# First token tile's layer norm in two groups of two blocks, and the first weights' low parts on GpSimd

## The chip, the core and the metric

The kernel runs on one core of a Trainium2 chip. The metric is the device time of one execution in microseconds (us). A core has a matmul engine (PE, TensorE), three engines for element-wise work (DVE = VectorE, ACT = ScalarE, POOL = GpSimd) and SyncE (SP), whose queue issues most of the transfers here. Each engine works through its own instructions in order, and waits at an instruction until all that it needs is there.

## The reference, cut to what matters

`x` is 2048 tokens by 640. It is normalised once, and the result goes both to an attention with 32 heads of 128 over 512 cached keys, and to a dense layer with a squared relu of width 1728. The output is gated.

```python
xn = _layernorm(x, axis=-1)                 # (x - mean) / sqrt(var + 1e-5)
q = xn @ wq                                 # 32 heads of 128
s = softmax(q @ k.T * 128 ** -0.5) @ v @ wo # per head, the last 512 cached positions
h = relu(xn @ w1 + b1) ** 2
g = silu(h @ w2 + b2)
return x + s * g
```

All arrays are float32.

## The kernel before

PE multiplies in a rounded float32 type (`F32R`). To keep the accuracy, each operand is kept as two tensors: a high part, which is a copy rounded by ACT (`activation(hi, src, AF.Copy)`), and a low part, the difference to the source (`tensor_tensor(lo, src, hi, op=subtract)`). A product of two such operands is three matmuls (`products`, L92 to L97): high by high (L95), high by low (L96), low by high (L97).

The tokens are cut into four tiles of 512 (`NT`), and each tile into four blocks of 128 rows. First the dense layer runs over tiles 0 to 2, each over 14 chunks of the width 1728 (13 of 128 and one of 64, which stands fourth). The attention follows, over all four tiles; the dense layer of tile 3 is spread over it. Attention is written out by a plan of due times that the change does not touch.

**The first tile.** `ln_first` (L200) calls `ln_stats(0)` (L132): four transfers of `x` (L144), and on DVE the statistics of each block (`bn_stats` in two halves, `bn_aggr`). After the fourth block, for all four at once, epsilon is added, ACT takes the square root (L154), and DVE makes the reciprocal and one Newton step of four small instructions. Then DVE normalises the four blocks in place. PE transposes them, 20 times 128x128, into five banks `px0` to `px4` (L205). `load_w(0, dve)` loads and splits the weights of chunk 0. ACT copies each bank to the high part `xT` (L210), DVE takes the low part; these ten instructions feed the first up-projection. For tiles 1 and 2, `ln_stats` and `ln_chunk` do the same work in another form during the tile before.

**The weights.** The weights of a chunk are loaded while tile 0 runs and stay. `load_w(f)` (L218) issues the transfer of the chunk's `w1` (to `w1r`, L221) and of its `w2` (to `w2r`, L226) on SP; then ACT makes the high parts (L231, L233) and an engine, DVE in every case, the low parts (L232, L234). `w1r` and `w2r` share a pool tag with two buffers, so the `w1r` of a chunk may be issued only when the `w1r` of the chunk before has been read by both engines, and `w2r` likewise.

**The first tile's loop.** `mlp_step(n)` emits the up-projection of chunk n and then the down-projection of chunk n-1. Up (`ph`): 15 matmuls, then ACT's relu `r` (L278), GpSimd's square (L237), ACT's high part `h` (L238) and DVE's low part (L239). Down (`py`): 15 matmuls that read h and `w2`.

**The order of the instructions.** An engine that is wrapped in `Ordered` (`pe`, `dve`, `act`, `pool`, `sp`; all its calls are recorded at L72) keeps the order in which the program states its instructions. Calls by `nc.` names are placed by a scheduler between them, by its own estimates. In `ln_first` before, DVE's work is ordered; ACT's, PE's and SP's is placed.

Of the kernel before, what the change touches and what calls it, by code (L numbers as in the profile page):

```python
# [8 lines left out]
F32 = mybir.dt.float32  # L9
F32R = mybir.dt.float32r  # L10
AF = mybir.ActivationFunctionType
# [3 lines left out]
P = 128  # L15
# [5 lines left out]
def kernel(  # L21
# [67 lines left out]
    def raw(ap):  # L89
        return ap.bitcast(F32)  # L90
# [39 lines left out]
    def ln_tile(t, b):  # L130
        tag = "stage" if t or b < 2 else "mr"
        return xp.tile([P, D], F32, tag=tag, name=f"xb{t}_{b}")  # L132

    def ln_stats(t):
# [24 lines left out]
        dve.tensor_tensor(r, r, y, op=ALU.mult)  # L159
        if t == 0:  # L160
            for b in range(NB):
                dve.tensor_scalar(
                    xn[b],
                    xn[b],
                    mv[:, 0, b : b + 1],
                    mv[:, 1, b : b + 1],
                    op0=ALU.subtract,
                    op1=ALU.mult,
                )
        xs = [  # L170
# [4 lines left out]
        ]  # L175
        return xn if t == 0 else mv, xs

# [22 lines left out]
    def ln_first():  # L200
        xn, xs = ln_stats(0)
        pts = [ps_y.tile([P, NT], F32, tag="py", name=f"px0_{c}") for c in range(DC)]
        for b in range(NB):
            for c in range(DC):
                nc.tensor.transpose(  # L205
                    pts[c][:, b * P : (b + 1) * P], xn[b][:, c * P : (c + 1) * P], ident
                )
        load_w(0, dve)
        for c in range(DC):
            nc.scalar.activation(xs[0][:, c, :], pts[c], AF.Copy)  # L210
            dve.tensor_tensor(xs[1][:, c, :], pts[c], raw(xs[0][:, c, :]), op=ALU.subtract)
        return xs
# [4 lines left out]

    def load_w(f, engine=nc.vector):  # L218
        f0, n = chunks[f]
# [5 lines left out]
        for k in range(0, P, n):  # L225
            nc.sync.dma_start(wb[k : k + n, :], w2[f0 : f0 + n, :])  # L226
        if n < P:
            w1p = [w1s[f][0][:, :, i * n : (i + 1) * n] for i in range(2)]
        else:
            w1p = w1s[f]  # L230
        nc.scalar.activation(w1p[0], wa[:, :, :n], AF.Copy)  # L231
        engine.tensor_tensor(w1p[1], wa[:, :, :n], raw(w1p[0]), op=ALU.subtract)  # L232
        nc.scalar.activation(w2s[f][0], wb, AF.Copy)  # L233
        engine.tensor_tensor(w2s[f][1], wb, raw(w2s[f][0]), op=ALU.subtract)  # L234

# [797 lines left out]
```

## Time and profile before

| | |
|---|---|
| time, median of 3 runs | 2020.71 us (2017.9 to 2021.19) |
| time of the profiled execution | 2021.47 us |
| its span, first to last instruction | 2019.7 us |
| granted TensorE clock, mean | 0.999 |
| busy: PE, DVE, POOL, ACT | 98%, 76%, 68%, 49% of the span |
| first transpose; first matmul of the up-projection | 12.53; 16.90 us |

A row of the timeline has the start, the length (both in us), the engine, the line, the operation, what it writes and reads with its shape, and in brackets how long the engine was idle before it and what ended that. A row of the waits has who waited for whom, the sum in us, how often, and the longest. A row of the windows has the window and its length, the busy time of PE, weight load, DVE, ACT and POOL with the number of instructions, the granted clock, the share of the transfer engines and GB/s. Rows of groups have the count, then the busy time and the mean in ns.

### The profile page before, as it was taken

The page shows a single profiled execution, that of the slowest core. Times are in us where ns is not written, and L with a number is a line of the kernel's source. Part 1 is how long each engine was busy: PE and PEld are TensorE (multiplying, and loading weights), DVE is VectorE, ACT ScalarE, POOL GpSimd, SP SyncE. Part 2 cuts the span into 40 slices and gives each one's busy share as a digit, 9 for nine tenths or more (in the row PEclk, how much of TensorE's full clock was granted, in tenths as well). Part 3 has the DMA queues.
Part 4 walks back from the last instruction along what each step waited for, and adds up shares of the span by engine and source line. Part 5 has one row for each costly group of instructions (what it writes and reads, how often), then busy time and mean ns, then how long its engine had stood idle before and what let it go on. Part 6 is the DMA issues. An engine that isn't in the chain of part 4 may idle for free.

```text
span 2019.7 us, 25025 instructions
## 1 busy us (share of the span) xinstructions
PE 1987.9 (98%) x8832; PEld 1609.3 (80%) x8832; DVE 1535.8 (76%) x2252; ACT 985.8 (49%) x1266; POOL 1375.4 (68%) x754
## 2 busy tenths in 40 slices
PE   7999999999999999999999999999999999999998
PEld 6788887788888888888887788787878888788877
DVE  5532337788888888888887778888888888888864
ACT  4432335555555555555554455555555555555533
POOL 1121227788777777777777788788888888877841
PEclk9999999999999999999999999999999999999999
DMA  4431454322333332333335433333333333333344
GB/s 140 128 113 29 177 196 132 99 90 89 90 89 89 90 89 90 90 91 90 91 96 159 154 95 105 110 110 111 110 110 111 110 112 110 96 91 90 106 146 140
DMA packets 126862, 220.32 MB, mean 109 GB/s; under 512 B 21542, under 2 KB 36304, under 8 KB 125456
## 3 DMA queue, kind: packets, MB, share of 16 engines
q1 hardware_dynamic: 123744, 204.28, 33.6%
q0 software_dynamic: 2992, 14.43, 1.8%
q8 instruction: 70, 1.15, 0.2%
q14 instruction: 56, 0.46, 0.1%
HBM read 194.26 MB, written 24.39 MB: 108 GB/s over the span
## 4 chain that ended last, share of the span: by engine, by line
PE 88%; DMA 6%; DVE 2%; POOL 1%; ACT 1%; issue 1%; SPq 0%; POOLq 0%; DVEq 0%
PE pq L72 20%; PE r L72 19%; PE s L72 17%; PE o L72 15%; DMA bm<-m_d 2%; PE py L96 2%; PE py L97 2%; PE py L95 2%; PE ph L96 2%; PE ph L95 2%; PE ph L97 2%; PE ly L72 2%; DMA m_d<-rowm 1%; PE lu L72 1%; DMA w1r<-in_w_dram 1%; DVE e L72 1%
## 5 line engine op out<-in xcount | busy, mean ns | idle before, releaser
L72 POOL TENSOR_TENSOR pt<-e,pt 128x1024 fp32r<-128x1024 f32 x256 | 617.5, 2412 | 296.1 <-ACT pt L72 296.1
L72 PE MATMUL r<-ot,wo 128*128 128x512 f32 x1920 | 496.9, 389 | 0.5 <-DVE acc L72 0.5
L72 PE MATMUL pq<-ax,wq 128*128 128x512 f32 x1920 | 473.1, 396 | 0.1
L72 ACT ACTIVATE e<-e 128x1024 f32<-128x1024 f32 x256 | 269.5, 1053 | 370.6 <-DVE e L72 331.6
L72 PEld LDWEIGHTS r<-ot,wo 128*128 128x128 f32 x1920 | 360.2, 188 | 75.9 <-DVE acc L72 0.9
L72 PEld LDWEIGHTS pq<-ax,wq 128*128 128x128 f32 x1920 | 350.9, 188 | 84.5 <-DMA ax<-xT_d 0.9
L72 PE MATMUL o<-pt,wv 128*128 128x512 f32 x1536 | 386.5, 398 | 0.4 <-POOL pt L72 0.3
L72 PE MATMUL s<-q,wk 128*128 128x512 f32 x1536 | 372.2, 391 | 9.1 <-DVE e L72 9.0
L72 DVE TRANSPOSE_TENSOR_REDUCE rdm<-s 128x32 f32<-128x1024 f32 x256 | 319.3, 1249 | 60.6 <-PE s L72 46.3
L72 PEld LDWEIGHTS s<-q,wk 128*128 128x128 f32 x1536 | 286.4, 188 | 76.9 <-DVE e L72 16.3
L72 PEld LDWEIGHTS o<-pt,wv 128*128 128x128 f32 x1536 | 278.7, 188 | 70.8 <-POOL pt L72 1.5
L72 DVE TENSOR_TENSOR e<-s,bm 128x1024 f32<-128x1024 f32 x256 | 299.9, 1212 | 37.5 <-DMA bm<-m_d 33.7
L72 POOL TENSOR_TENSOR su<-e,e 128x1024 f32<-128x1024 f32 x128 | 308.5, 2410 | 0.0
L72 ACT ACTIVATE pt<-e 128x1024 fp32r<-128x1024 f32 x256 | 271.7, 1061 | 7.8
L72 DVE TENSOR_TENSOR acc<-r,acc 128x512 f32<-128x512 f32 x300 | 202.5, 675 | 2.8 <-PE r L72 2.8
L237 POOL TENSOR_TENSOR r<-r 128x512 f32<-128x512 f32 (+1 forms) x42 | 44.1, 1049 | 227.5 <-ACT r L278 207.9
L72 ACT ACTIVATE ot<-o 128x512 fp32r<-128x512 f32 x128 | 76.8, 600 | 228.3 <-DVE o L72 228.3
L72 DVE TRANSPOSE_TENSOR_REDUCE rds<-su 128x32 f32<-128x1024 f32 x128 | 158.5, 1239 | 10.7 <-POOL su L72 9.0
L72 ACT ACTIVATE q<-pq 128x512 fp32r<-128x512 f32 x128 | 76.7, 599 | 164.8 <-PE pq L72 164.7
L72 DVE TENSOR_TENSOR ot<-o,ot 128x512 fp32r<-128x512 f32 x128 | 88.5, 691 | 32.0 <-ACT ot L72 32.0
L239 DVE TENSOR_TENSOR h<-r,h 128x512 fp32r<-128x512 f32 (+1 forms) x42 | 29.0, 690 | 107.7 <-ACT h L238 107.6
L72 POOL TENSOR_TENSOR wq<-qr,wq 128x640 fp32r<-128x640 f32 x62 | 98.5, 1588 | 4.0 <-ACT wq L72 2.8
(122 smaller groups left out, 2152.6 us busy)
## 6 DMA issues: line engine op xcount, KB each, us to landing
bm<-m_d SPq DMA_DIRECT2D x128, 256.0 KB, 3.3
bs<-s_d SPq DMA_DIRECT2D x128, 256.0 KB, 4.0
qr<-in_wq_dram SPq DMA_DIRECT2D x64, 320.0 KB, 4.4
or<-in_wo_dram SPq DMA_DIRECT2D x64, 320.0 KB, 4.5
kr<-in_kT_dram SPq DMA_DIRECT2D x64, 256.0 KB, 4.4
vr<-in_v_dram SPq DMA_DIRECT2D x64, 256.0 KB, 4.3
xT_d<-xT POOLq DMA_DIRECT2D x6, 1280.0 KB, 7.5
xb<-in_x_dram SPq DMA_DIRECT2D x16, 320.0 KB, 3.5
```

The lines of the kernel that those rows point to most:

```text
L72: ins = method(*args, **kwargs)
L95: nc.tensor.matmul(ps, ah, bh, start=first and i == 0, stop=False)
L96: nc.tensor.matmul(ps, ah, bl, start=False, stop=False)
L97: nc.tensor.matmul(ps, al, bh, start=False, stop=last and i == n - 1)
L237: nc.gpsimd.tensor_tensor(r, r, r, op=ALU.mult)
L239: nc.vector.tensor_tensor(lo, r, raw(hi), op=ALU.subtract)
```

## The change

In `ln_first`, the statistics of the first tile are now taken in two groups of two blocks. Epsilon, root, reciprocal and Newton step run once for each group, on half as many columns. The Newton step of group 0 runs on GpSimd, that of group 1 on DVE. Group 0 is normalised and transposed between the statistics of block 2 and block 3. All of it is ordered now, on DVE, ACT, POOL, PE and SP. A square root of a constant is taken at the start (`warm`).

`load_w` is cut in two: `load_w_raw` (the transfers) and `split_w` (high and low part). For chunk 0 the low parts of `w1` and `w2` are made by GpSimd in place of DVE, and ACT's high parts are ordered; the transfers are stated ahead of the layer norm. Other chunks call both parts as before.

The scheduler places the rest anew. In the changed program, ACT converts the `w1` of chunk 1 ahead of the five copies `xT`, and DVE takes its low part ahead of the five differences; PE has the biases' transpose between the two groups, and the first matmul of chunk 1's up-projection directly behind the first of chunk 0's. On SP, the `w1` of chunk 1 now comes ahead of the first two blocks of tile 1, and its `w2` behind them. Some relus and h of tile 0 change places with the weights' conversions next to them: `r1` then stands behind both conversions of chunk 2, `r2` behind chunk 4's `w1`, `r4` behind chunk 7's `w1`, `h7` behind chunk 11's `w2`. From the second tile on, every engine has the order of before.

```diff
--- before.py
+++ after.py
@@ -157,23 +157,13 @@
         dve.tensor_tensor(r, r, var, op=ALU.mult)
         dve.tensor_scalar(r, r, -0.5, 1.5, op0=ALU.mult, op1=ALU.add)
         dve.tensor_tensor(r, r, y, op=ALU.mult)
-        if t == 0:
-            for b in range(NB):
-                dve.tensor_scalar(
-                    xn[b],
-                    xn[b],
-                    mv[:, 0, b : b + 1],
-                    mv[:, 1, b : b + 1],
-                    op0=ALU.subtract,
-                    op1=ALU.mult,
-                )
         xs = [
             keep.tile([P, DC, NT], F32R, tag="acc", name=f"xT{t}_{i}", bufs=2)
             if t % 2
             else xp.tile([P, DC, NT], F32R, tag=f"xT{i}", name=f"xT{t}_{i}", bufs=1)
             for i in range(2)
         ]
-        return xn if t == 0 else mv, xs
+        return mv, xs
 
     def ln_rows(t, mv, xs):
         pm = psx.tile([P, NT], F32, tag="x", name=f"pmv{t}")
@@ -198,16 +188,69 @@
         nc.vector.tensor_tensor(xs[1][:, c, :], xc, raw(xs[0][:, c, :]), op=ALU.subtract)
 
     def ln_first():
-        xn, xs = ln_stats(0)
+        mv = xp.tile([P, 4, NB], F32, tag="mv", name="mv0")
+        sc = xp.tile([P, 3, NB], F32, tag="sc", name="sc0")
+        sts = [xp.tile([P, 2, 6], F32, tag="st", name=f"st0_{b}", bufs=4) for b in range(NB)]
+        MV = [mv[:, :2, 2 * k : 2 * k + 2] for k in range(2)]
+        SCR = [[sc[:, i, 2 * k : 2 * k + 2] for i in range(3)] for k in range(2)]
+        warm = sc[:, 2, :1]
+        pool.memset(warm, 1.0)
+        act.activation(warm, warm, AF.Sqrt)
+        xn = []
+        for b in range(NB):
+            xb = ln_tile(0, b)
+            sp.dma_start(xb, x[b * P : (b + 1) * P, :])
+            xn.append(xb)
+        raws = load_w_raw(0)
         pts = [ps_y.tile([P, NT], F32, tag="py", name=f"px0_{c}") for c in range(DC)]
-        for b in range(NB):
-            for c in range(DC):
-                nc.tensor.transpose(
-                    pts[c][:, b * P : (b + 1) * P], xn[b][:, c * P : (c + 1) * P], ident
-                )
-        load_w(0, dve)
+        xs = [
+            xp.tile([P, DC, NT], F32R, tag=f"xT{i}", name=f"xT0_{i}", bufs=1) for i in range(2)
+        ]
+        hd, n = D // 2, NB // 2
+
+        def stats(k, j):
+            st = sts[n * k + j]
+            for i in range(2):
+                dve.bn_stats(st[:, i, :], xn[n * k + j][:, i * hd : (i + 1) * hd])
+            dve.bn_aggr(MV[k][:, :, j], st)
+
+        def root(k):
+            var, sd, _ = SCR[k]
+            dve.tensor_scalar(var, MV[k][:, 1, :], EPS, None, op0=ALU.add)
+            act.activation(sd, var, AF.Sqrt)
+
+        def newton(k, eng):
+            var, sd, y = SCR[k]
+            r = MV[k][:, 1, :]
+            dve.reciprocal(y, sd)
+            eng.tensor_tensor(r, y, y, op=ALU.mult)
+            eng.tensor_tensor(r, r, var, op=ALU.mult)
+            eng.tensor_scalar(r, r, -0.5, 1.5, op0=ALU.mult, op1=ALU.add)
+            eng.tensor_tensor(r, r, y, op=ALU.mult)
+
+        def normalise(k):
+            for b in range(n * k, n * k + n):
+                m, q = (MV[k][:, i, b - n * k : b - n * k + 1] for i in range(2))
+                dve.tensor_scalar(xn[b], xn[b], m, q, op0=ALU.subtract, op1=ALU.mult)
+                for c in range(DC):
+                    pe.transpose(
+                        pts[c][:, b * P : (b + 1) * P], xn[b][:, c * P : (c + 1) * P], ident
+                    )
+
+        stats(0, 0)
+        stats(0, 1)
+        root(0)
+        newton(0, pool)
+        stats(1, 0)
+        normalise(0)
+        split_w(0, raws, pool, 0)
+        stats(1, 1)
+        root(1)
+        split_w(0, raws, pool, 1)
+        newton(1, dve)
+        normalise(1)
         for c in range(DC):
-            nc.scalar.activation(xs[0][:, c, :], pts[c], AF.Copy)
+            act.activation(xs[0][:, c, :], pts[c], AF.Copy)
             dve.tensor_tensor(xs[1][:, c, :], pts[c], raw(xs[0][:, c, :]), op=ALU.subtract)
         return xs
 
@@ -215,7 +258,7 @@
         for i in range(2):
             pool.dma_start(xT_d[t][i][:, cs, :], raw(xs[i])[:, cs, :])
 
-    def load_w(f, engine=nc.vector):
+    def load_w_raw(f):
         f0, n = chunks[f]
         wa = xp.tile([P, DC, P], F32, tag="stw", name=f"w1r{f}", bufs=2)
         nc.sync.dma_start(
@@ -224,14 +267,23 @@
         wb = xp.tile([P, D], F32, tag="stw", name=f"w2r{f}", bufs=2)
         for k in range(0, P, n):
             nc.sync.dma_start(wb[k : k + n, :], w2[f0 : f0 + n, :])
-        if n < P:
-            w1p = [w1s[f][0][:, :, i * n : (i + 1) * n] for i in range(2)]
+        return wa[:, :, :n], wb
+
+    def split_w(f, raws, engine, k):
+        n = chunks[f][1]
+        if k:
+            hi, lo = w2s[f]
+        elif n < P:
+            hi, lo = (w1s[f][0][:, :, i * n : (i + 1) * n] for i in range(2))
         else:
-            w1p = w1s[f]
-        nc.scalar.activation(w1p[0], wa[:, :, :n], AF.Copy)
-        engine.tensor_tensor(w1p[1], wa[:, :, :n], raw(w1p[0]), op=ALU.subtract)
-        nc.scalar.activation(w2s[f][0], wb, AF.Copy)
-        engine.tensor_tensor(w2s[f][1], wb, raw(w2s[f][0]), op=ALU.subtract)
+            hi, lo = w1s[f]
+        (act if f == 0 else nc.scalar).activation(hi, raws[k], AF.Copy)
+        engine.tensor_tensor(lo, raws[k], raw(hi), op=ALU.subtract)
+
+    def load_w(f, engine=nc.vector):
+        raws = load_w_raw(f)
+        for k in range(2):
+            split_w(f, raws, engine, k)
 
     def square_split(r, hi, lo):
         nc.gpsimd.tensor_tensor(r, r, r, op=ALU.mult)
```

## The prediction

> **What bounds the kernel now.** I read the page's busy shares first, then PE's waits, then the windows by stage.
>
> ```profile
> span 2019.7 us, 25025 instructions
> PE 1987.9 (98%) x8832; PEld 1609.3 (80%) x8832; DVE 1535.8 (76%) x2252; ACT 985.8 (49%) x1266; POOL 1375.4 (68%) x754
> PE px L205 <- DVE xb L72: 12.5, 1, 12.5
> PE s L72 <- DVE e L72: 9.0, 13, 1.8
> 50.00:110.00 60.00, 58.88 (x256) 47.40 (x256) 31.76 (x57) 23.64 (x37) 9.68 (x9) 1.00 0.38 108
> 110.00:210.00 100.00, 100.00 (x443) 82.40 (x442) 29.50 (x56) 30.92 (x46) 19.46 (x22) 1.00 0.21 72
> ```
>
> PE is busy in all but 31.8 of 2019.7 us. Of these, 12.5 are one wait at the start, for the first normalised tile; 9.0 lie in the attention, which the change leaves as it is; 1.1 lie between 50 and 110 us, in the first token tile, while the weights still arrive (60.00 less 58.88). From 110 us on PE doesn't pause. So the change can pay only by what it takes from the 12.5 us and the pauses of the first tile, and that must then reach the end behind a PE that is never idle for long.
>
> The start, from the timeline:
>
> ```profile
> 5.67 0.21 DVE L72 BATCH_NORM_AGGREGATE mv<-st 128x2 f32<-128x12 f32 x1
> 5.95 0.89 DVE L72 BATCH_NORM_STATS2 st<-xb 128x6 f32<-128x320 f32 x2
> 8.48 0.74 ACT L231 ACTIVATE w1s<-w1r 128x640 fp32r<-128x640 f32 x1 [6.46 <-DMA w1r<-in_w_dram]
> 8.69 0.17 DVE L72 TENSOR_SCALAR sc<-mv 128x4 f32<-128x4 f32 x1
> 9.23 1.28 ACT L154 ACT_TABLE_LOAD   x1
> 10.53 0.21 ACT L154 ACTIVATE sc<-sc 128x4 f32<-128x4 f32 x1
> 11.78 2.18 DVE L72 TENSOR_SCALAR xb<-xb,mv 128x640 f32<-128x640 f32 x4
> 12.53 4.50 PE L205 MATMUL px<-ident,xb 128*128 128x128 f32 x20 [12.53 <-DVE xb L72]
> 13.88 0.82 DVE L72 TENSOR_TENSOR w1s<-w1r,w1s 128x640 fp32r<-128x640 f32 x1
> 14.61 0.82 DVE L72 TENSOR_TENSOR w2s<-w2r,w2s 128x640 fp32r<-128x640 f32 x1
> 14.76 0.38 SPq L221 DMA_DIRECT2D w1r<-in_w_dram  x1
> 16.22 2.56 ACT L210 ACTIVATE xT<-px 128x512 fp32r<-128x512 f32 x5 [4.86 <-PE px L205]
> 16.85 3.08 DVE L72 TENSOR_TENSOR xT<-px,xT 128x512 fp32r<-128x512 f32 x5 [1.42 <-ACT xT L210]
> 16.90 0.78 PE L95 MATMUL ph<-xT,w1s 128*128 128x512 f32 x1
> 17.59 0.79 PE L96 MATMUL ph<-xT,w1s 128*128 128x512 f32 x1
> 18.59 0.39 PE L95 MATMUL ph<-xT,w1s 128*128 128x512 f32 x1
> 19.27 0.74 ACT L231 ACTIVATE w1s<-w1r 128x640 fp32r<-128x640 f32 x1 [0.49 <-DMA w1r<-in_w_dram]
> 20.89 0.38 SPq L221 DMA_DIRECT2D w1r<-in_w_dram  x1
> ```
>
> One serial chain: four blocks' statistics and the variance, ready at 8.86; it waits until 10.53 for ACT, which converts a weight and loads the square root's table; the reciprocal and four Newton steps from 10.74 to 11.78 (five small steps, 0.2 each); normalising; twenty transposes of 0.225 us to 17.03; the copies xT from 16.22; the second product at 17.59. The load of chunk 1's w1 is issued at 14.76, when DVE has read chunk 0's, and lands at 19.25, when ACT's wait for it ends.
>
> **Part by part.** *Group 0 and the warm-up.* One table load (1.28) goes, since the square root's comes first, in ACT's wait for the first weight that ends at 8.46. Blocks 0 and 1 have their statistics at 5.88, add, root and reciprocal (0.17, 0.21, 0.2 and small gaps) end near 6.5. The four Newton steps on GpSimd have no row of this size; the nearest bound one from below and above:
>
> ```profile
> L1016 POOL MEMSET const-float32-0.0<- 128x1 f32 x1 | 0.1, 99 | 0.2 <-issue 0.2
> masks.py:199 POOL TENSOR_SCALAR_AFFINE_SELECT ident<-ident 128x128 f32<-128x128 f32 x1 | 0.3, 295 | 0.1
> L72 POOL TENSOR_TENSOR wq<-qr,wq 128x640 fp32r<-128x640 f32 x62 | 98.5, 1588 | 4.0 <-ACT wq L72 2.8
> w1r<-in_w_dram SPq DMA_DIRECT2D x13, 320.0 KB, 3.3
> br<-in_b_dram POOLq DMA_DIRECT2D x1, 2.5 KB, 5.4
> ```
>
> That is 0.4 to 1.2 us; I take 0.9, by the middle of the two, to 7.45. Block 2's statistics on DVE (0.89 and 0.21, from 6.55 to 7.67) hide it; at 1.2 it still ends by 7.75, and without that cover DVE would stand for its whole length. Two normalisings, 2.18/4 = 0.545 each, end at 8.8, and ten transposes (2.25) end near 10.5, before group 1 needs PE. The biases' transpose now stands between the groups; its last load takes 5.4 from its issue, which GpSimd makes before it has anything of group 0 to do; even from 5.88 it lands by 11.3, before group 1's first transpose.
>
> *Group 1.* Block 3's statistics run from 8.8 to 9.9, root and reciprocal to 10.5, DVE's four Newton steps (0.2 each) to 11.3, normalising to 12.4. Ten transposes end at about 14.2, px0 at 13.3. By that alone the copies xT would start 2.9 us earlier than 16.22.
>
> *The low parts on GpSimd.* ACT's first high part ends at 9.22 as before; GpSimd subtracts until 9.25 + 1.59 = 10.84, and SP issues chunk 1's w1 at 10.9, not 14.76: 3.9 earlier. In SP's order it now comes before both blocks of the next tile, which follow it at once, and chunk 1's w2. GpSimd's next work behind them is the first square, which has to wait for the whole first up-projection, so nothing there is held.
>
> *The wait that decides the start.* In the changed program's order ACT converts chunk 1's w1 **ahead** of the five copies xT, and DVE takes its low part **ahead** of the five xT differences. Before, both stood behind. So the copies wait for this load. Such a load takes 3.3 at the median of the first 110 us and took 4.49 among other loads (14.76 to 19.25): it lands between 14.2 and 15.4. I take 3.6, nearer the median because it is first in its burst: 14.5. ACT's conversion ends at 15.25; DVE's low part starts at 15.27 and DVE is free for the next after 0.73 (13.88 to 14.61): the first xT difference starts at 16.0 in place of 16.85. PE's second product comes 0.85 earlier (0 to 1.15 by the two ends). The one product of chunk 1 that now stands between PE's first two fits in their pause.
>
> *GpSimd beside DVE.*
>
> ```profile
> 59.43 1.10 POOL L237 TENSOR_TENSOR r<-r 128x512 f32<-128x512 f32 x1 [4.06 <-ACT r L278]
> 59.55 1.00 DVE L72 TENSOR_TENSOR mv<-mv,sc 128x4 f32<-128x4 f32 x1
> 60.79 0.16 DVE L72 TENSOR_TENSOR mv<-mv,sc 128x4 f32<-128x4 f32 x1
> ```
>
> The same DVE step took 1.00 while GpSimd ran, and 0.16 alone: it ended when GpSimd did. In the changed kernel GpSimd's two subtractions (9.25 to 10.84, and from about 11.1, behind ACT's second high part, to 12.7) lie over group 1's Newton steps and normalising. If these wait for both, normalising starts at 12.7 and px0 is ready at 14.6; still under 15.25, so the sum stands. "SBUF: State Buffer" of the Trainium skill (Who interferes with whom) says that a VectorE op with two SBUF inputs, or in a two-port mode, fully blocks against a GpSimd op. By that rule the add of epsilon may wait too, and px0 comes near 15.4: 0.2 us more, 2018.7 in all. The trace agrees for two inputs; no row shows the one-input case.
>
> *PE's slow first products.* From 17.59 to 18.59 two products took 0.50 each, where the 443 of the window from 110 us took 0.226 each, although transposes had run since 12.53. When it turns fast in the changed kernel no row tells. If at the same moment, the 0.85 shrinks by some 0.2 to 0.4; if 1.7 after the first product, as here, by nothing. I take 0.1. "TensorE: Matmul & The Clock Gate" of the Trainium skill (Part 1) speaks of a free-running window of 3.4 us; by it the turn could come up to 1.7 later, at half rate some 0.8 more: 2019.3.
>
> *What the first tile makes of it.* PE now waits for late h four times, each behind a weight:
>
> ```profile
> 50.32 0.50 PE L96 MATMUL py<-h,w2s 128*128 128x512 f32 x1 [0.16 <-DVE h L239]
> 64.76 0.50 PE L96 MATMUL py<-h,w2s 128*128 128x512 f32 x1 [0.39 <-DVE h L239]
> 68.80 0.74 ACT L231 ACTIVATE w1s<-w1r 128x640 fp32r<-128x640 f32 x1 [1.22 <-DMA w1r<-in_w_dram]
> 69.45 0.67 ACT L278 ACTIVATE r<-ph,b_sb 128x512 f32<-128x512 f32 x1
> 72.01 0.50 PE L95 MATMUL py<-h,w2s 128*128 128x512 f32 x1 [0.35 <-ACT h L238]
> 72.74 0.50 PE L96 MATMUL py<-h,w2s 128*128 128x512 f32 x1 [0.22 <-DVE h L239]
> L221 SPq DMA_DIRECT2D w1r<-in_w_dram x14: 367/379/433, 2.6 to 75.2; - x14
> 58.23 4.25 DMA w2r<-in_w_dram
> ```
>
> 1.1 us idle, and up to 0.16 more each, since a matmul's row lasts 0.39 (18.59) at a pitch of 0.23: some 1.8 in all. At 69.45 the relu runs only because the weight at 68.80 has been converted. So until about 73 us two legs run: PE's, now 0.75 earlier and with up to 1.8 of pauses to lose, 2.5 in all; and the loads', 14 of them over 75 us, each issued when the last has been read. Their lead is 3.9 at chunk 1 and 4.8 at chunk 2 (the low part ends at 16.1 in place of 20.87), but each later conversion also stands behind a relu or an h that moves only with PE. At chunk 11 the lead lies between PE's 0.75 and 3.9. I take 2.2, just under the middle, as the h of 72.01 now stands behind a second weight. The smaller leg counts: 2.2, with 0.7 and 2.8 as its ends. Behind it PE is never idle until the attention, so it arrives.
>
> Sum: 2021.47 of the profiled execution less 2.2 is 2019.3. That execution lies 0.76 over the median of the runs shown (2020.71), so I predict 2018.5.
>
> **The rivals.** *The whole head start.* If the copies xT started when px0 is ready, 2.9 earlier, with all 1.8 of the pauses gone, the gain is 4.7: 2016.0. For it: the leg of PE allows it. Against: the load issued at 10.9 would have to land by 12.5, in 1.6 us against 3.3. It needs the conversion not to hold the copies.
>
> *The start gains, and it is lost.* The attention's own waits (9.0 us in 13) shift by a microsecond or two with the moment at which loads meet, and PE's slow phase may last longer: gain about 0.25, 2020.5. For it: the three runs already differ by 3.3. Against: 100 us of PE without a pause follow the first tile.
>
> *Slower: weights ahead of relus.* In ACT's new order r4 stands behind chunk 7's w1, before behind chunk 6's w2; r1 and r2 are also moved behind one more weight. If loads take 4.25, as one did, in place of 3.3, the six loads from chunk 2 to 7 come 5.7 late. With a lead of 2.2, less one more conversion (0.74), h4 comes 1.46 earlier; PE asks for it 0.75 earlier, and it was late by 0.16 + 0.16 (50.32): slack 0.4. PE would stand 5.3 at the fifth down-projection; less the 0.75 and the 1.8 that vanish, 2.75 slower: 2023.5. It decides from half a microsecond more per load, where 6 x 0.5 less 0.4 makes up the 2.55. Against: the median of 3.3 is over these very loads, and they still have a lead.
>
> **How the numbers follow.** The likeliest (0.7 to 2.8 earlier) gets 0.60, the whole head start 0.12, lost again 0.18, slower 0.10. A measurement of this kernel tells about 0.2% from no change, 4.0 us. The likeliest case lies inside it; with the runs' scatter 0.06 of it goes beyond, and with nine tenths of the head start faster gets 0.17. Of the slower case half goes past 4 us by scatter and longer waits, of the lost one a tenth: 0.07. The same gets 0.76. The range takes the likeliest's 2017.9 to 2020.0, the rivals down to 2016.0 and up to 2020.5, and a scatter of about 1: 2015.6 to 2021.9.
>
> **What would show it.** Right: one table load before 12 us; chunk 1's w1 issued near 10.9; ACT idle until it lands and the xT copies straight behind its conversion, near 15.3; group 1's normalising stretched by GpSimd; the second product near 16.8; PE's pauses of 50 to 73 us mostly gone, and the same product of 72.74 at about 70.5. Wrong: xT copies starting at 13.3 (the order didn't matter), a PE pause near 49 us of several microseconds (weights held the relus), or a start that is earlier with a span that isn't.

## The result, and the profile of the changed kernel

| | before | changed |
|---|---|---|
| median | 2020.16 us (22 runs) | 2016.14 us (22 runs) |
| ratio, 95% interval | 1 | 0.9981 (0.9975 to 0.9988) |
| profiled execution, its span | 2021.47, 2019.7 us | 2017.95, 2016.2 us |
| predicted | | 2018.5 us, 2015.6 to 2021.9 |

The change gained 0.19% (0.12 to 0.25%), 4.0 us between the medians. Measured twice more, with 27 runs of before each time, the same pair gave 0.9988 (0.9979 to 0.9997) and 0.9986 (0.9977 to 0.9995).

PE's waits in the changed kernel, in the columns of the prediction's rows (who waited for whom, us, times, longest):

```profile
PE px L72 <- DVE xb L72: 11.1, 2, 8.4
PE s L72 <- DVE e L72: 8.1, 10, 1.9
```

And the window from 50 to 110 us of the changed kernel:

```profile
50.00:110.00 60.00, 60.00 (x266) 49.32 (x265) 31.36 (x55) 23.33 (x36) 9.55 (x9) 1.00 0.36 102
```

The wait at the start shrank from 12.5 to 11.1 us. The pauses of the first tile are gone: PE is busy for all 60 us, where it was for 58.88. The attention's waits (`s` for `e`) are 8.1 us, where they were 9.0. So two places can have paid in the first tile, its start and its pauses. Which one did is seen in the start, from the changed kernel's timeline:

```profile
0.73 1.28 ACT L72 ACT_TABLE_LOAD   x1 [0.73 <-PEq L1068]
6.65 0.19 POOL L72 TENSOR_TENSOR mv<-sc 128x2 f32<-128x2 f32 x1 [2.90 <-DVE sc L72]
7.48 0.19 POOL L72 TENSOR_TENSOR mv<-mv,sc 128x2 f32<-128x2 f32 x1
8.96 1.54 POOL L72 TENSOR_TENSOR w1s<-w1r,w1s 128x640 fp32r<-128x640 f32 x1 [1.29 <-ACT w1s L72]
9.92 0.61 DVE L72 TENSOR_SCALAR sc<-mv 128x2 f32<-128x2 f32 x1
10.53 0.38 SPq L264 DMA_DIRECT2D w1r<-in_w_dram  x1
11.46 1.53 POOL L72 TENSOR_TENSOR w2s<-w2r,w2s 128x640 fp32r<-128x640 f32 x1 [0.96 <-ACT w2s L72]
11.59 1.42 DVE L72 TENSOR_TENSOR mv<-mv,sc 128x2 f32<-128x2 f32 x1
13.05 1.14 DVE L72 TENSOR_SCALAR xb<-xb,mv 128x640 f32<-128x640 f32 x2
13.59 0.74 ACT L280 ACTIVATE w1s<-w1r 128x640 fp32r<-128x640 f32 x1 [2.20 <-DMA w1r<-in_w_dram]
13.72 2.40 PE L72 MATMUL px<-ident,xb 128*128 128x128 f32 x10 [2.73 <-DVE xb L72]
15.30 2.56 ACT L72 ACTIVATE xT<-px 128x512 fp32r<-128x512 f32 x5 [0.98 <-PE px L72]
16.97 0.63 PE L96 MATMUL ph<-xT,w1s 128*128 128x512 f32 x1
19.93 0.39 PE L97 MATMUL ph<-xT,w1s 128*128 128x512 f32 x1
23.59 0.63 ACT L290 ACTIVATE h<-r 128x512 fp32r<-128x512 f32 x1 [1.15 <-POOL r L289]
```

The copies `xT` start at 15.30, not 16.22, and the second product at 16.97, not 17.59. But the first high part `h` comes at 23.59. Before it came here:

```profile
23.40 0.63 ACT L238 ACTIVATE h<-r 128x512 fp32r<-128x512 f32 x1 [1.16 <-POOL r L237]
```

It is 0.19 us *later* than before. Between 16.97 and 19.53 PE's products start 0.43 apart, from 19.93 on 0.23; before, they are 0.23 apart from 18.59 on. The head start is spent there. What was gained came behind it. The high part `h` of tile 1's first chunk (the fifteenth in the kernel) stands at 114.32, and at 116.46 before, 2.14 us earlier. Two more rows show how, PE's windows from 25 to 110 us (busy us and, in brackets, matmuls), first before, then the changed kernel:

```profile
25.00:110.00 85.00, 83.88 (x366) 1.00 0.40 113
```

```profile
25.00:110.00 85.00, 85.00 (x375) 1.00 0.39 111
```

PE makes nine more matmuls in the same 85 us. At 0.227 each that is 2.0 us: the 1.12 us of idle time and the slower restarts around it. So the first tile's gain of 2.14 is -0.19 from the start and 2.33 from what lies between the two `h`, the pauses in the main. The reason for the pause at 64.76 is in ACT's order. Before, and then the same weight in the changed kernel:

```profile
58.68 0.67 ACT L278 ACTIVATE r<-ph,b_sb 128x512 f32<-128x512 f32 x1
62.50 0.74 ACT L233 ACTIVATE w2s<-w2r 128x640 fp32r<-128x640 f32 x1 [3.15 <-DMA w2r<-in_w_dram]
63.15 0.61 ACT L238 ACTIVATE h<-r 128x512 fp32r<-128x512 f32 x1
```

```profile
58.92 0.74 ACT L280 ACTIVATE w2s<-w2r 128x640 fp32r<-128x640 f32 x1 [1.25 <-DMA w2r<-in_w_dram]
59.57 0.67 ACT L330 ACTIVATE r<-ph,b_sb 128x512 f32<-128x512 f32 x1
61.45 0.63 ACT L290 ACTIVATE h<-r 128x512 fp32r<-128x512 f32 x1 [1.21 <-POOL r L289]
...
66.81 0.74 ACT L280 ACTIVATE w1s<-w1r 128x640 fp32r<-128x640 f32 x1 [2.68 <-DMA w1r<-in_w_dram]
69.33 0.63 ACT L290 ACTIVATE h<-r 128x512 fp32r<-128x512 f32 x1
```

Before, `h6` (63.15), which PE needs at once, stands behind chunk 9's `w2`, which PE doesn't need before `h9` (82.23 in the changed kernel), and ACT stands 3.15 us until that weight has landed. In the changed kernel the weight stands ahead of `r6` instead, and `h6` waits only for GpSimd's square. That order costs `r6` little (59.57 for 58.68), because the weight is converted 3.6 us earlier (58.92 for 62.50). The pauses of 72.01 and 72.74 go by an earlier weight alone: in both kernels the relu of chunk 7 stands behind chunk 11's `w1`, which is converted at 66.81 in place of 68.80.

### The profile page after: what moved, and what is told of

The parts are those of the page before. It is cut to its first block, busy times and chain, and to the rows that moved or that the text cites. A ratio compares the mean times of both kernels' runs of the same rounds, so it can differ in the third digit from the quotient of the medians.

```text
span 2016.2 us, 25037 instructions
## 1 busy us (share of the span) xinstructions
PE 1988.1 (99%) x8832; PEld 1610.2 (80%) x8832; DVE 1534.7 (76%) x2252; ACT 985.0 (49%) x1267; POOL 1378.5 (68%) x761
## 4 chain that ended last, share of the span: by engine, by line
PE 90%; DMA 5%; DVE 2%; POOL 1%; issue 1%; ACT 1%; SPq 0%; POOLq 0%
PE pq L72 20%; PE r L72 19%; PE s L72 17%; PE o L72 15%; PE ph L95 2%; PE ph L96 2%; PE py L96 2%; PE ph L97 2%; PE py L95 2%; PE py L97 2%; DMA bm<-m_d 2%; PE ly L72 2%; DMA m_d<-rowm 1%; PE lu L72 1%; DVE e L72 1%
```

## The experiments

Each ratio is against runs of before on the same chip, beside that kernel. The measures are in one table: the ratio, the first `h`, the `h` of tile 1's first chunk, the time between the two, PE's matmuls from 25 to 110 us, and what stands behind chunk 9's `w2` on ACT (profiled executions, all but the ratio).

| kernel | ratio (95%) | first h | tile 1 | between | matmuls | behind the w2 |
|---|---|---|---|---|---|---|
| before | 1 | 23.40 | 116.46 | 93.06 | 366 | h6 |
| before, again | (one run) | 23.62 | 116.09 | 92.47 | 368 | h6 |
| changed | 0.9981 (0.9975-0.9988) | 23.59 | 114.32 | 90.73 | 375 | r6 |
| changed, again | 0.9988 (0.9979-0.9997) | 23.43 | 114.47 | 91.04 | 373 | r6 |
| changed, third | 0.9986 (0.9977-0.9995) | 23.68 | 114.54 | 90.86 | 374 | r6 |
| low parts alone | 1.0007 (0.9998-1.0017) | 24.29 | 117.67 | 93.38 | 363 | r6 (h6 behind chunk 10's) |
| copies first | 0.9995 (0.9985-1.0004) | 24.08 | 116.88 | 92.80 | 367 | h6 |
| w2's low part on VectorE | 0.9991 (0.9982-1.0) | 22.43 | 115.08 | 92.65 | 368 | h6 |
| both low parts on VectorE | 0.9992 (0.9983-1.0001) | 25.02 | 115.81 | 90.79 | 374 | r6 |
| clock warmed | 0.998 (0.9971-0.9989) | 21.84 | 114.28 | 92.44 | 368 | r6 |
| relus first | 1.0005 (0.9996-1.0014) | 23.53 | 116.30 | 92.77 | 366 | written out |
| all three | 0.9984 (0.9975-0.9993) | 21.83 | 114.90 | 93.07 | 365 | written out |
| all three, late root | 0.9979 (0.997-0.9988) | 24.43 | 116.09 | 91.66 | 372 | written out |
| before, relus first | 0.9989 (0.998-0.9998) | 23.10 | 114.89 | 91.79 | 371 | written out |

The first `h` also depends on when PE turns fast, which differs from execution to execution (between 16.05 and 20.92 us in the runs without additional matmuls); the time between the two `h` begins behind that. Some expectations below put tile 1's first relu, or its first `h`, at 114.7 and 116.9; the rows of the `h` have 114.32 and 116.46. The leads are meant, and they are read here from the `h`.

### Do the copies wait for chunk 1's weight?

**Copies first.** The changed kernel with chunk 1's conversions stated behind the copies:

```diff
             act.activation(xs[0][:, c, :], pts[c], AF.Copy)
             dve.tensor_tensor(xs[1][:, c, :], pts[c], raw(xs[0][:, c, :]), op=ALU.subtract)
+        load_w(1, dve)
...
-        (act if f == 0 else nc.scalar).activation(hi, raws[k], AF.Copy)
+        (act if f <= 1 else nc.scalar).activation(hi, raws[k], AF.Copy)
...
-            if t == 0 and f > 0:
+            if t == 0 and f > 1:
                 load_w(f)
```

> The changed kernel with chunk 1's conversions ordered behind the copies xT (ACT) and behind the xT differences (DVE). The prediction's step: the copies wait for chunk 1's w1. Then they should start about 0.7 or more earlier than the 15.30 us of the changed kernel, and the first difference, freed of the low part ahead of it, near 15.0 (15.93). Theory 'GpSimd': the copies wait for the transposes, which wait for a normalising that GpSimd's second low part holds (one Newton step of 1.42 us at 11.59). Then the copies start at 15.1 to 15.4 as in the changed kernel, and the first difference at 15.7 to 16.0; the loads of chunk 2 start up to 5 us later (15.21 in the changed kernel), and tile 1 starts up to 1 us later than there.

From its timeline:

```profile
12.35 1.42 DVE L72 TENSOR_TENSOR mv<-mv,sc 128x2 f32<-128x2 f32 x1
13.81 1.14 DVE L72 TENSOR_SCALAR xb<-xb,mv 128x640 f32<-128x640 f32 x2
16.06 2.56 ACT L72 ACTIVATE xT<-px 128x512 fp32r<-128x512 f32 x5 [3.91 <-PE px L72]
```

With nothing ahead of them on ACT, the copies start at 16.06, still behind `px`. Normalising starts 0.76 later than in the changed kernel (13.81 for 13.05; the first weight landed 0.76 later in this execution), and so do the copies (16.06 for 15.30). So in the changed kernel the order of copies and conversion doesn't decide when the copies start: they wait for DVE's normalising, and this waits for GpSimd. Chunk 2's `w1` is issued at 20.53 in place of 15.21, `h6` stands behind chunk 9's `w2` as before, and the pauses are back: tile 1 comes 2.56 later than in the changed kernel, where 1 at most was expected.

**w2's low part on VectorE.** If GpSimd's second subtraction holds the normalising, it must start earlier without it. In the changed kernel:

```diff
         root(1)
-        split_w(0, raws, pool, 1)
+        act.activation(w2s[0][0], raws[1], AF.Copy)
         newton(1, dve)
         normalise(1)
+        dve.tensor_tensor(w2s[0][1], raws[1], raw(w2s[0][0]), op=ALU.subtract)
```

> The changed kernel, with chunk 0's second low part (w2) on DVE behind group 1's normalising in place of GpSimd. Theory 'GpSimd': the Newton step of 1.42 us falls to 0.16, group 1's normalising starts at 11.8 (13.05), px0 is ready near 13.9, and the copies xT start at 14.35, when chunk 1's w1 has been converted (15.30 in the changed kernel): the first product near 15.0 and the second near 15.7 (15.95 and 16.97). The prediction's step (the copies wait for chunk 1's w1 alone): the copies don't move, 15.2 to 15.4. In time at most 1 us under the changed kernel, which the timing can hardly tell.

```profile
9.93 1.14 DVE L72 TENSOR_SCALAR sc<-mv 128x2 f32<-128x2 f32 x1
12.13 0.16 DVE L72 TENSOR_TENSOR mv<-mv,sc 128x2 f32<-128x2 f32 x1
12.33 1.14 DVE L72 TENSOR_SCALAR xb<-xb,mv 128x640 f32<-128x640 f32 x2
14.23 0.74 ACT L281 ACTIVATE w1s<-w1r 128x640 fp32r<-128x640 f32 x1 [2.30 <-DMA w1r<-in_w_dram]
14.87 2.53 ACT L72 ACTIVATE xT<-px 128x512 fp32r<-128x512 f32 x5
```

The last Newton step takes 0.16 in place of 1.42, normalising starts at 12.33 (11.8 expected; the add of epsilon still ends with GpSimd's first subtraction), and now the copies do stand directly behind chunk 1's conversion, at 14.87. So the wait that the prediction named exists; in the changed kernel it was hidden behind a longer one. The first `h` comes 1.16 us earlier: the second product 0.44 (16.53 for 16.97), the rest because products turn fast at 18.11 here, at 19.93 there. The pauses came back, here too with chunk 2's load issued at 19.38 and `h6` behind the `w2`; of 1.16 us, tile 1 gets nothing (115.08).

**Both low parts on VectorE**, the change without its GpSimd part:

```diff
-        split_w(0, raws, pool, 0)
+        split_w(0, raws, dve, 0)
...
-        split_w(0, raws, pool, 1)
+        split_w(0, raws, dve, 1)
```

> The changed kernel with both low parts of chunk 0 on VectorE in place of GpSimd, everything else kept: the change without its GpSimd part. Theory 1 (GpSimd's second low part blocks VectorE and so sets the copies; on VectorE the two parts cost 1.5 of its own time, and chunk 1's w1, loaded from 9.8 and converted by 13.6, has its low part ahead of group 1's normalising): copies near 16.6 (16.2 to 17.0), 1.3 later than in the changed kernel, first h near 24.6, tile 1's first relu 0.8 to 1.8 us ahead of before, no blocked small step on VectorE. Theory 2 (blocking does not matter, the table load and the split into groups give all of it): copies at 15.3 as in the changed kernel and tile 1's first relu 2.0 ahead.

```profile
14.20 0.83 DVE L281 TENSOR_TENSOR w1s<-w1r,w1s 128x640 fp32r<-128x640 f32 x1 [0.19 <-ACT w1s L280]
14.94 1.13 DVE L72 TENSOR_SCALAR xb<-xb,mv 128x640 f32<-128x640 f32 x2
17.18 2.55 ACT L72 ACTIVATE xT<-px 128x512 fp32r<-128x512 f32 x5 [3.02 <-PE px L72]
```

No small step is blocked, but DVE makes the low parts itself, chunk 1's too, ahead of the normalising: copies at 17.18, 1.9 later than in the changed kernel (1.3 expected), first `h` 1.43 later. Yet from there to tile 1 it takes 90.79 us, as the changed kernel does, and not a pause is in it. Against the two runs of before tile 1 is 0.3 and 0.65 us earlier (0.8 to 1.8 expected). This run starts latest of all fourteen, and still tile 1 begins before it does in the kernel before (115.81 for 116.09). The start and the gain are two things.

**Low parts alone**: before with `load_w(0, pool)` in place of `load_w(0, dve)`.

> The kernel before, with chunk 0's two low parts on GpSimd and nothing else. Chunk 1's w1 should be issued near 10.9 us (before 14.76), but GpSimd's subtractions now lie over DVE's Newton steps and normalising, and ACT has both conversions of chunk 1 ahead of the copies xT: these should start near 17.4 (before 16.22), the first up-projection about 1.2 later than before. Theory 'loads': the gain of the change comes in the main from earlier loads, which take away PE's pauses between 50 and 80 us. Then tile 1 starts 0.3 to 1.4 earlier than before (its first h 116.9 us in the profile before, 114.7 after), although the first product is later, and the time is 0 to 2 us under before. Theory 'start': the gain is the earlier first product. Then tile 1 starts about 1 later than before and the time is 1 us above it.

```profile
11.53 1.41 DVE L72 TENSOR_TENSOR mv<-mv,sc 128x4 f32<-128x4 f32 x1
```

GpSimd blocks the last Newton step here too, the copies start at 17.20 and the first `h` is 0.9 later. The load of chunk 1's `w1` is issued at 10.81 and of chunk 2's at 16.57, both four us earlier than before, and it brings nothing: PE still stands 1.1 us in three pauses between 65 and 74, tile 1 comes 1.2 later, and 1.0007 is no gain, as theory 'start' has it. ACT converts one chunk further ahead here, and `h6` stands behind chunk 10's `w2`, for which ACT waits 3.30 us. An early start of the loads, with an `h` still behind a weight, was worth nothing.

### What the slow products cost

**Clock warmed.** The changed kernel with six matmuls on the first weight, whose result is not used:

```diff
         newton(1, dve)
+        pw = psx.tile([P, NT], F32, tag="x", name="pw")
+        wt = w1s[0][0].rearrange("p c n -> p (c n)")
+        for _ in range(6):
+            pe.matmul(pw, wt[:, :P], wt[:, :NT], start=True, stop=True)
```

> The changed kernel with six matmuls more, whose result is not used, on PE between the transposes of the two groups (chunk 0's rounded w1 times itself, 128x128 by 128x512), in the 2.7 us in which PE waits. Theory: PE's slow phase in the first up-projection (0.43 us a product until 19.5 in the changed kernel) ends earlier, since these products count as work where transposes don't: the first products take 0.23 at once or soon, the first h starts 0.8 to 1.2 earlier (23.59), and tile 1 starts 0.5 to 1.2 earlier (114.7), unless the loads then hold PE between 45 and 75 us. Rival: the phase ends by the time since the kernel's start or since the transposes: no change, 23.4 to 23.8.

```profile
10.54 2.02 PE L72 MATMUL pw<-w1s 128*128 128x512 f32 x6
14.18 1.31 PE L72 MATMUL px<-ident,xb 128*128 128x128 f32 x10 [1.62 <-DVE xb L72]
16.47 0.50 PE L96 MATMUL ph<-xT,w1s 128*128 128x512 f32 x1 [0.23 <-DVE xT L72]
16.81 0.39 PE L97 MATMUL ph<-xT,w1s 128*128 128x512 f32 x1
```

Ten transposes take 1.31 in place of 2.40, no product is slow, and the first `h` comes 1.75 us earlier (21.84). So the slow phase cost the start more than the whole layer norm had won.

The theory of the expectation has it that transposes don't count as work for the clock. Two other runs contradict it. The twenty transposes of *low parts alone*, and then of *before, relus first* (below), without any additional matmul:

```profile
13.74 3.86 PE L205 MATMUL px<-ident,xb 128*128 128x128 f32 x20 [13.74 <-DVE xb L72]
12.82 3.95 PE L205 MATMUL px<-ident,xb 128*128 128x128 f32 x20 [12.82 <-DVE xb L72]
```

Before, they took 4.50. In both runs the first ones start 0.21 apart and the last five 0.11, and no product behind them is slow: PE turned fast among transposes. In the fourteen executions it did so about 3 to 6.2 us after it had begun to work with hardly a pause, whatever the work. So the six matmuls can do what they do by filling the 2.73 us in which PE stood ahead of group 1; that their kind matters isn't shown.

But tile 1 starts at 114.28, as in the changed kernel: `h6` and `h7` come at 61.53 and 69.28 there, at 61.45 and 69.33 in the changed kernel, behind the same weights at nearly the same times. PE arrives 1.75 earlier and waits, and ACT waits for the weight ahead of `r6`, 2.42 us, where in the changed kernel it was 1.25:

```profile
59.00 0.74 ACT L284 ACTIVATE w2s<-w2r 128x640 fp32r<-128x640 f32 x1 [2.42 <-DMA w2r<-in_w_dram]
62.94 0.50 PE L96 MATMUL py<-h,w2s 128*128 128x512 f32 x1 [0.23 <-DVE h L295]
```

The ratio of 0.998 isn't told apart from the changed kernel's.

### What sets the end of the first tile

**The pair again on one chip.** Both kernels unchanged, to see whether the attention adds to the 2.14.

> The kernel before, unchanged, profiled on the chip of the next three runs, so that the attention can be compared on one chip. What is open: the median fell by 4.0 us, the first tile hands only 2.1 us to the second. Theory A (the first tile is the whole effect, the rest is how loads meet in the attention of one execution): after tile 1's first relu the traces of before and changed stay within 1.5 us of their lead there, either way. Theory B (the attention itself became shorter by about 2 us): the changed kernel gains another 1.3 us or more between tile 1's first relu and the end. First tile as in the profile of before: table load between 9 and 11, xT copies near 16.2, pauses of PE near 65, 72 and 73.

> The changed kernel, unchanged, on the same chip. Ratio 0.998 by both theories. Tile 1's first relu 2.1 us earlier than in the profile of before taken with it (1.7 to 2.5); from there to the end Theory A: lead changes by less than 1.5 us either way; Theory B: it grows by 1.3 us or more. xT copies near 15.3, behind px, and the one-input add of epsilon ending with GpSimd's first low part.

Tile 1's first `h` is 1.62 us earlier (116.09 to 114.47; 1.7 to 2.5 was expected) and the last instruction 1.5 (spans 2014.1 and 2012.6). Between them the lead, from the same instruction of ACT in both traces, moved between 0.1 and 2.6: theory A. The waits of PE in the attention (`s` for `e`) came to 5.2 us in this execution of before and 5.9 in this one of the changed kernel, 9.0 and 8.1 in the first pair: they differ more between executions than between the kernels.

**The change a third time**, beside two kernels of the last group:

> The changed kernel, unchanged, beside the next two kernels. Two measurements so far: 0.9981 (0.9975 to 0.9988) and 0.9988 (0.9979 to 0.9997). If the gain is what the first tile hands on, 1.6 to 2.1 us, the ratio is about 0.999 (0.9988 to 0.9992); if the attention becomes shorter besides, 0.998.

0.9986 is between the two expectations and tells them not apart; tile 1's first `h` is at 114.54, and PE waits 8.4 us in the attention.

**Relus first.** ACT's order in the first tile's loop written out: the weights of chunk f+1 come between `h` of chunk f-1 and the relu of chunk f. In the changed kernel:

```diff
         normalise(1)
+        first.append(load_w_raw(1))
+        split_w(1, first[0], dve, 0)
         for c in range(DC):
...
-        nc.scalar.activation(r, ph, AF.Relu, bias=b1_sb[:, f : f + 1])
+        scalar = act if t == 0 else nc.scalar
+        scalar.activation(r, ph, AF.Relu, bias=b1_sb[:, f : f + 1])
...
-            if t == 0 and f > 0:
-                load_w(f)
+            if t == 0 and f == 0:
+                split_w(1, first[0], nc.vector, 1)
+            elif t == 0 and f + 1 < FC:
+                load_w(f + 1)
```

(`h` and the halved chunk likewise, and every conversion by `act`.)

> The changed kernel with ACT's order in the first tile written out: the weights of chunk f+1 are converted between h of chunk f-1 and the relu of chunk f, so that no relu stands behind a weight further ahead. Theory 1 (what ends the first tile is ACT's order, with relus and h behind weights several chunks ahead that are still loading): no pause of PE over 0.1 us between 25 and 110 us, also none near 59 to 73. Since the changed kernel has hardly any pauses there, tile 1's first relu then comes within 0.4 us of the changed kernel's, and the ratio to before is 0.998, as for the change. Theory 2 (the rate of loads itself bounds the first tile): with fewer chunks in advance the loads come late, PE waits at the up-projections for w1s, and tile 1's first relu comes later than in the changed kernel by over 1 us.

```profile
54.00 0.21 ACT L154 ACTIVATE sc<-sc 128x4 f32<-128x4 f32 x1 [7.05 <-DVE sc L72]
54.11 0.72 ACT L72 ACTIVATE w1s<-w1r 128x640 fp32r<-128x640 f32 x1
54.88 0.50 PE L95 MATMUL ph<-xT,w1s 128*128 128x512 f32 x1 [1.45 <-ACT w1s L72]
```

The pauses from 59 to 73 are gone, and a new one is there: the square root of tile 1's statistics fell ahead of chunk 6's weights, ACT waited 7.05 us for it, and PE 1.45 for the weight, whose conversion had no transfer to wait for. Neither theory had this. Tile 1 starts 1.83 later than in the changed kernel on the same chip (116.30 for 114.47), and the ratio is 1.0005.

**All three**: this order, the six matmuls, and `w2`'s low part on VectorE behind chunk 1's.

> The kernel of the run before this one, and in addition six matmuls on the first weight ahead of group 1's transposes, whose result is not used, and the low part of chunk 0's w2 on VectorE behind chunk 1's w1. Theory 1 (start and pauses each cost on their own, and ACT's order was what gave the start back): first h near 21.3 (22.43 and 21.84 with one of the two alone), no pauses until 110 us, tile 1's first relu 4.3 us earlier than in the profile of before taken with it (3.6 to 5.0), so about 2.2 us faster than the changed kernel: ratio 0.9968 (0.996 to 0.9977). Theory 2 (loads bound the exit from the first tile): pauses of PE near 59 to 73 come back, tile 1's first relu is 2.0 to 2.3 us earlier than in before whatever the start, ratio 0.998.

First `h` at 21.83, 1.6 earlier than in the changed kernel on this chip, and the same pause, 1.72 at 53.49: tile 1 at 114.90, no earlier than there. The ratio of 0.9984 (0.9968 expected) isn't told apart from the changed kernel's 0.9988.

**All three, late root**: the same with tile 1's statistics stated behind the sixth up-projection.

```diff
-            if f == ln_stats_at:
+            if f == ln_stats_at and t:
                 LN[t + 1] = ln_stats(t + 1)
...
             HS[n] = up(t, f, XS[t])
+            if f == ln_stats_at and not t:
+                LN[t + 1] = ln_stats(t + 1)
```

> The kernel with ACT's order written out, the clock warmed and w2's low part on VectorE, and with tile 1's statistics emitted behind the sixth up-projection, so that their square root no longer stands ahead of a weight's conversion. In the run before PE waited 1.72 and 0.19 us near 53 for that weight, since the square root waited 7 us for VectorE. Theory 1 (that pause was the whole of what was lost after the start): no pause of PE over 0.1 us from 25 to 110 us; tile 1's first relu 3.0 us earlier than in the before profiled with that run (2.6 to 3.6), 1.2 earlier than the changed kernel on the same chip; ratio 0.998 or a little lower, under the changed kernel's by 0.0006. Theory 2 (with fewer chunks in advance some other wait comes next): another pause of over 1 us before 110 us, no gain over the changed kernel.

The pause shrank to 0.30 and 0.19 (at 61.52 and 62.44). But in this execution PE's clock, fast from 14.20 on, fell back. The last two rows are PE's windows, with the granted clock behind the matmuls:

```profile
15.77 0.50 PE L95 MATMUL ph<-xT,w1s 128*128 128x512 f32 x1 [0.74 <-ACT xT L72]
17.48 0.70 PE L96 MATMUL ph<-xT,w1s 128*128 128x512 f32 x1 [1.21 <-DVE xT L72]
14.20:17.61 3.41, 1.47 (x10) 1.00 0.52 169
17.61:21.02 3.41, 3.41 (x9) 0.50 0.52 165
```

Between the transposes and the products PE paused twice, 0.74 and 1.21 us, for copies and differences that stand behind chunk 1's weight. It worked 1.47 of 3.41 us, and for the next 3.41 the clock was 0.50. In *all three*, with 0.33 and 1.21 (1.86 of work from 13.18 to 16.59), no product is slow. The first `h` is 2.6 later than there. 0.9979 is the lowest ratio of all, and its interval holds that of the changed kernel on the same chip: that it beats the change isn't shown.

**Before, relus first.** The kernel before, its layer norm untouched, with ACT's order written out and the late root. If the change's gain lies in ACT's order, this must show it.

> The kernel before with its first layer norm unchanged, and only ACT's order in the first tile's loop written out (weights of chunk f+1 between h of chunk f-1 and the relu of chunk f; tile 1's statistics emitted behind the sixth up-projection). Theory 1 (what the change gained at the first tile is ACT's new order behind the start, not the layer norm: in before, and in every run with pauses near 64 to 73, h6 stood behind chunk 9's w2): first h at 23.4 to 23.9 as in before, no pauses from 60 to 75 but the one of 0.3 to 0.5 near 61 for the square root, PE's products from 25 to 110 within 4 of the changed kernel's 375 to 377, tile 1's first relu 0.7 to 1.8 us earlier than in before, ratio 0.9991 to 0.9997. Theory 2 (the loads' lead of four us from GpSimd's low part is needed as well): PE waits for weights at the up-projections, over 1.5 us in sum, and tile 1's first relu is not earlier than in before.

```profile
16.37 2.56 ACT L210 ACTIVATE xT<-px 128x512 fp32r<-128x512 f32 x5 [4.73 <-PE px L205]
23.10 0.63 ACT L72 ACTIVATE h<-r 128x512 fp32r<-128x512 f32 x1 [1.16 <-POOL r L238]
60.32 0.50 PE L95 MATMUL ph<-xT,w1s 128*128 128x512 f32 x1 [0.48 <-ACT w1s L72]
```

The copies start at 16.37, as before. The pauses from 64 to 73 are gone; 0.66 us near 60 and 61 are left. Tile 1 starts 1.20 us earlier than in the second run of before (on another chip), of which 0.52 were there at the first `h`, as the copies start 0.27 earlier and no product is slow; 0.68 lie behind it, 1.27 against the first run of before. The ratio is 0.9989 (0.998 to 0.9998): about the change's, without a single edit of the layer norm. Its weights are even loaded later than before (the load of chunk 8's `w1` starts at 61.21; in the second run of before at 49.69). Theory 1 holds for this order. What isn't separated is whether the other order, which the scheduler made in the changed kernel, pays without the early loads too: in each run in which that order freed `h6` of a weight, chunk 2's `w1` was issued by 15.8.

## Why the prediction was right, and where it was wrong

The sign was right, the time lies in the range, and what the first tile hands on came near the forecast (2.2 predicted, 2.14 and 1.62 measured). The gain in time, 3.8 us by the ratio (2.4 to 5.0), is larger than the 2.2 predicted. And the sum was made of other parts than predicted.

- *Group 0 and the warm-up.* Right: one table load before 12 us, four Newton steps on GpSimd from 6.65 to 7.67 (1.02 with their gaps, 0.9 predicted), hidden by block 2's statistics; transposes done at 10.8 for 10.5.
- *Low parts on GpSimd.* Right: chunk 1's `w1` is issued at 10.53 (10.9 predicted).
- *The wait that decides the start.* **Wrong.** It said that the copies wait for chunk 1's weight, which lands at 14.5. ACT's wait for the weight ended at 13.59, 3.06 after its issue, and it was converted by 14.33; the copies waited another 0.98 for `px`. What decides is GpSimd's second low part (11.46 to 12.99), which holds the last Newton step until 13.01. The predicted 15.25 and the measured 15.30 agree by chance: *copies first* shows that the named wait costs the copies nothing, *w2's low part on VectorE* that it comes next when the other is taken away.
- *GpSimd beside DVE.* The prediction had this blocking, with normalising at 12.7 (13.05 measured), and put it just under the bound of the load. The first of the two subtractions blocked as well: the add of epsilon, one input, took 0.61 and ended with GpSimd at 10.53; in other runs it took 1.14 and 1.32; alone it takes 0.17. "SBUF — State Buffer" of the Trainium skill (Who interferes with whom) has `tensor_scalar` among the operations that can contend with GpSimd. The trace agrees, and the prediction's 15.4 for px0 by this rule is near the 15.30 at which the copies start behind it. The statistics, at 0.88 beside GpSimd and 0.89 alone, aren't held.
- *PE's slow first products.* **Mis-sized**: 0.1 was taken; it cost the 0.62 of head start, and 0.19 more. The first fast product stands 4.0 after the first (19.93), where before it was 1.7 (18.59). The change cuts PE's transposes in two, and PE's work begins anew at 13.72, where before it ran through from 12.53. How much of the delay is due to this, and how much to the chance of an execution, isn't separated: the turn came at 19.34 and 19.82 in the other two executions of the changed kernel, at 18.57 in the second of before, but among the transposes in *low parts alone* and *before, relus first*. *Clock warmed* puts the whole phase at 1.75 us at least, since normalising started 0.46 later in that execution (13.51). "TensorE: Matmul & The Clock Gate" of the Trainium skill (Part 1) has a free-running window of 3.4 us. The trace agrees in the length: in *all three, late root* the clock is full for 3.41 us, then 0.50 for 3.41. The prediction's estimate of 0.8 by that page was nearer than the value taken.
- *What the first tile makes of it.* That the smaller of two legs counts is borne out, and the legs' sums came near: PE's leg, predicted as 0.75 + 1.8, was -0.19 + 2.33 (0.19 + 1.43 in the second pair of profiles); the loads' at chunk 11, predicted as 2.2, was 2.0 (the conversion of 68.80 moved to 66.81). In *clock warmed* PE's leg was shortened by 1.75 us, and tile 1 moved by 0.04: the loads' leg then bounds. What the prediction did not see is what this leg is made of: a weight that lands late holds PE through ACT's order, with an `h` or a relu behind a weight several chunks ahead. It listed the relus that moved behind weights, and took only a loss from it, not that `h6` had come out from behind one.
- *The rivals.* The whole head start failed, as the copies didn't start at 13.3. Weights ahead of relus, slower, failed: no pause of PE near 49 us. That the start gains and loses again came true of the start itself, by the slow products and not in the attention; its 2020.5 did not, as the pauses went.

What stays open is why the gain in time (3.8, 2.4 and 2.8 us by the three ratios; 4.0, 2.9 and 3.6 between the medians) is more than the 1.6 to 2.1 that the first tile hands on. The intervals reach down to 2.4, 0.6 and 1.0 us, and the 22 runs of the changed kernel alone range over 7.4 us. In the first pair of profiles the lead grew from 2.14 at tile 1 to 3.5 at the end; in the pair that was profiled on the same chip it did not grow.

## What to carry to other kernels

When a gain at the start meets an engine that works in order, ask what stands between the two uses: here the order of conversions, relus and `h` on ACT gave the gain, together with loads that came early, and a change anywhere before it can shuffle that order. Measure the lead at several points (first `h`, middle, next tile); the same total can come from a part that no one had edited. And write out the order of an engine that serves both what is needed now and what is needed several steps on, then look what else of it, such as a square root that waits, falls into the new place.

## What the runs showed of the hardware

- PE turned fast about 3 to 6.2 us after it had begun to work with hardly a pause, in fourteen executions, and transposes count as work: in two of them it turned fast among the twenty transposes (3.86 and 3.95 us in all, 4.50 where it didn't). It fell back once, for 3.41 us, behind 3.41 us in which it had worked 1.47; with 1.86 in another execution it stayed fast.
- A VectorE step on 128x2 elements with one input took 0.61 to 1.32 us in place of 0.17 beside a GpSimd subtraction, and ended with it each time. A GpSimd step of that size takes 0.18 to 0.20 us, and one follows the other in 0.26 to 0.30.
